# Cosine attention with top-128 routing: seven consecutive tokens per partition, 64x64 transposes, and 128-wide tiles throughout

## The chip, the core and the metric

The kernel runs on one core of a Trainium2 chip, as one launch. The metric is the device time of that launch in microseconds (us). The engines that the text names are TensorE (PE in the profile; PEld is its weight loading), VectorE (DVE), ScalarE (ACT), GpSimd (POOL) and SyncE (SP), which here only issues transfers. SBUF is the on-chip memory and PSUM the memory that TensorE writes.

## The reference

Eight batches, twelve heads, 448 tokens and 64 numbers per head and token. The attention is a softmax over cosine similarities; its result, with the heads side by side (768 numbers per token), goes through a layer in which only the 128 tokens of each batch with the highest score are changed.

```python
q_n = q / (np.linalg.norm(q, axis=-1, keepdims=True) + 1e-06)
k_n = k / (np.linalg.norm(k, axis=-1, keepdims=True) + 1e-06)
scores = np.matmul(q_n, k_n.transpose(0, 1, 3, 2)) / tau          # tau = 0.1
attn = softmax(scores)                                            # over the keys
x = matmul(attn, v)  ->  (8, 448, 768)
for b in range(8):
    s = x[b] @ w_gate
    top = the 128 tokens with the largest s
    h = np.maximum(x[b, top] @ w1, 0.0)                           # w1: 768 x 1024
    out[b, top] = x[b, top] + sigmoid(s[top])[:, None] * (h @ w2) # w2: 1024 x 768
```

448 is three times 128 plus 64. That odd 64 is what the layouts in this case are about.

## The kernel before

Work is done for one pair of heads at a time; there are 48 pairs, six to a batch. The program is scheduled by hand, and each engine runs its instructions in the written order. With `P = 128, NC = 3, NS = 4, T = 64, NB7 = 7, E = 65`:

```python
def load(gi, which, eng):            # q, k or v of a group of up to three pairs
    ...
    if which == 0:                   # q: 1 transfer for tokens 0..383, 2 for the last 64
        eng.dma_start(out=..., in_=src[b, h0:h0+nh, 0:SM, :].rearrange("h (m c) d -> m h (c d)", c=NC))
        for u in range(2):
            eng.dma_start(out=dst[u*T:u*T+T, :, NC], in_=src[b, h0:h0+nh, SM:S, :]...)
        return
    for u in range(2):               # k and v: 4 transfers
        for half in range(2):
            ...
            eng.dma_start(...)
load(0, 0, nc.sync); load(0, 1, nc.scalar)
load(1, 0, nc.sync); load(1, 1, nc.scalar)
load(2, 0, nc.sync); load(2, 1, nc.scalar)
load(0, 2, nc.sync); load(1, 2, nc.sync); load(2, 2, nc.sync)
...
def square(p):  nc.scalar.activation(sq_tiles[p], raw q and k of the pair, AF.Square)    # L198
def sum_pe(p, dst):                  # eight matmuls with the identity: sums of squares   # L205
def sum_dve(p, dst):                 # the rest of the sum                                # L211
def scale(p): ...                    # kn = q, k over their norms, two POOL operations    # L235
def transposes(p, part):
    # part 0: four 64x64 transposes (the last 64 tokens of q, k, two heads)               # L255
    # part 1: six 128x128 transposes                                                      # L250
def qkT_copy(p): nc.vector.tensor_copy(qkT_tiles[p], qkT_ps[:, :W])                       # L269
def scores(i, c, sc=None):           # c = 0..2: one 128-key block, both heads            # L281
                                     # c = 3: the last 64 keys of both heads              # L286
def exps(i, c):                      # exp of a score block on ACT                        # L294, L297
def pv_tails(i):                     # 8 matmuls, 64 rows high                            # L308
    for j in range(NS):
        n = rows(j)                  # 128, and 64 for j = 3
        for u in range(2): matmul(out=o_ps[:n, u, ...], lhsT=ex[r, TAIL, j*P:j*P+n], rhs=vo[r, NC], ...)
def pv(i):                           # 24 matmuls                                         # L320
    for u in range(2):
        for j in range(NS):
            n = rows(j)
            for c in range(NC): matmul(out=o_ps[:n, u, ...], lhsT=ex[:, 2*c+u, j*P:j*P+n], ...)
def pv_evac(i): ...                  # x_b = o_ps / its sum, on DVE                       # L333, L334
def gate(b, j): ...                  # the token score x . w_gate, on DVE                 # L355
def rank_count, pick                 # rank of each token, 0/1 selection, on DVE          # L401, L410
def select(b):                       # 8 matmuls; for j = 3 with 64 rows                  # L420
def gather(b, part):                 # 24 matmuls in two parts; for j = 3 with 64 rows    # L456
def ffn1, ffn2                       # the two layers for the 128 chosen tokens           # L470, L479

for i in range(N + 1):               # the main loop: pair i, and the end of pair i - 1
    scores(i, 0); scores(i, 1)
    pv_tails(i - 1); pv(i - 1)
    exps(i, 0); exps(i, 1); square(...)
    run(i, "D1"); pv_evac(i - 1); run(i, "A"); run(i, "D2")   # D: gate, rank, pick; A: PE work
    scores(i, 2)
    transposes(i + 1, 0); transposes(i + 1, 1); qkT_copy(i + 1)
    sc = ps_sc.tile([P, 2, 512], FP32, name="sc")             # a pool of two buffers
    sums(sq, sc)                     # sum_pe into sc[:, 1], then sum_dve out of it
    scores(i, 3, sc)                 # into sc[:, 0]
    exps(i, 2); exps(i, 3)
    norms(sq)
    run(i, "C"); scale(i + 2); values(i + 2); run(i, "P2"); run(i, "B")   # B: PE work
```

`run` hands in the pieces of the routed layer of the batch before: gates at pairs 0 to 3 of the following batch, ranks at pair 5, gather and the two layers over pairs 6 to 10.

Of the kernel before, what the change touches and what calls it, by code (L numbers as in the profile page):

```python
# [17 lines left out]
def kernel(  # L18
# [51 lines left out]
    def rows(j):  # L70
        return P if j < NC else T
# [10 lines left out]
    while sum(NORMS[-1]) < N:  # L82
# [4 lines left out]
    raw = [(const.tile([P, 2, 3, 8, Dh], FP32, name=f"qk_raw{n}"),  # L87
            const.tile([P, 3, 8, Dh], FP32, name=f"v_raw{n}")) for n in range(NRAW)]

    def load(gi, which, eng):  # L90
        g0, gn = GROUPS[gi]
        b, hp = divmod(g0, HP)
        h0, nh = 2 * hp, 2 * gn
        qk, vr = raw[gi % NRAW]
        src = (q, k, v)[which]
        dst = vr[:, :gn] if which == 2 else qk[:, which, :gn]
        if which == 0:
            eng.dma_start(
                out=dst.rearrange("p g (u c) d -> p (g u) (c d)", c=4)[:, :, :NC * Dh],
                in_=src[b, h0:h0 + nh, 0:SM, :].rearrange("h (m c) d -> m h (c d)", c=NC))  # L100
            for u in range(2):
                eng.dma_start(
                    out=dst[u * T:u * T + T, :, NC],
                    in_=src[b, h0:h0 + nh, SM:S, :].rearrange(
                        "(g h) p d -> p g h d", h=2)[:, :, u])
            return


        for u in range(2):
            for half in range(2):  # L110
                n = NS if half == u else NC
                b0 = 0 if u == 0 else NB7 - n
                t0 = 0 if half == u else NS * T
                eng.dma_start(
                    out=dst[half * T:half * T + T, :, b0:b0 + n]
                    .rearrange("p g c d -> p g (c d)"),
                    in_=src[b, h0:h0 + nh, t0:t0 + n * T, :].rearrange(
                        "(g h) (p c) d -> p g h (c d)", h=2, c=n)[:, :, u])
# [7 lines left out]
    load(2, 1, nc.scalar)  # L126
    load(0, 2, nc.sync)
    load(1, 2, nc.sync)
    load(2, 2, nc.sync)
# [8 lines left out]
    nc.vector.memset(o_ps[T:, :, NC * E:NS * E], 1.0)  # L138
# [6 lines left out]
    kn = const.tile([P, 2, NS, P], BF16, name="qkn")  # L145
# [5 lines left out]
    for t in gates + ranks:  # L151
        nc.vector.memset(t, 0.0)
# [5 lines left out]
    for sl, col, base, step, mult in (  # L158
            (slice(0, NC), 0, 0, 0, NC - 1), (slice(0, NC), 1, 0, 1, 1),
            (slice(NC, NS), 0, SM, 0, 0), (slice(NC, NS), 1, 0, 0, 1)):  # L160
        nc.gpsimd.iota(tokc[:, sl, col], pattern=[[step, sl.stop - sl.start]],
                       base=base, channel_multiplier=mult,
                       allow_small_or_imprecise_dtypes=True)
# [9 lines left out]

    nc.gpsimd.tensor_copy(iden_f, iden_b)
    for j in range(NS):
        nc.gpsimd.affine_select(
            out=tie[:, j, :], in_=tie[:, j, :], compare_op=ALU.is_ge,
            fill=-(2.0 ** -126), base=-j * P, pattern=[[1, S]],
            channel_multiplier=-1)
# [12 lines left out]
    def square(p):  # L192
        gi, g = place[p]
        n, m = nplace[p]
        if m == 0:
            ss_tiles[n] = prep.tile([P, 3, 2, NB7], FP32, name="ss")
        sq_tiles[p] = prep.tile([P, 2, NB7 * Dh], BF16, name="sq")
        nc.scalar.activation(  # L198
            sq_tiles[p], raw[gi % NRAW][0][:, :, g].rearrange("p a b d -> p a (b d)")
            [:, :, :NB7 * Dh], AF.Square)  # L200
# [27 lines left out]
    def scale(p, engines=None):  # L228
        gi, g = place[p]
        n, m = nplace[p]  # L230
        qk = raw[gi % NRAW][0]
        rs = rs_tiles[n]
        for eng, b0, nb, o in zip(engines or (nc.gpsimd, nc.gpsimd),
                                  (0, NS), (NS, NC), (0, Dh)):
            eng.tensor_mul(  # L235
                kn[:, :, :nb, o:o + Dh], qk[:, :, g, b0:b0 + nb],
                rs[:, m, :, b0:b0 + nb].rearrange("p a (b o) -> p a b o", o=1)
                .to_broadcast([P, 2, nb, Dh]))

    def values(p):  # L240
        gi, g = place[p]
        nc.gpsimd.tensor_copy(vo_bufs[p % NB][:, :, :Dh], raw[gi % NRAW][1][:, g, :NB7])  # L242
# [3 lines left out]
    def transposes(p, part):  # L246

        def full(a, c):
            o = a * KO + c * P
            nc.tensor.transpose(out=qkT_ps[:, o:o + P], in_=kn[:, a, c], identity=iden_b)  # L250

        def tail(a, u):
            r = slice(u * T, u * T + T)
            o = SM if a == 0 else KT + u * T
            nc.tensor.transpose(out=qkT_ps[r, o:o + T], in_=kn[r, a, NC, :Dh],  # L255
                                identity=iden_b[r, r], tile_position=(u * T, u * T))

        if part == 0:
            for a in range(2):
                for u in range(2):  # L260
                    tail(a, u)
        else:
            for a in range(2):
                for c in range(NC):
                    full(a, c)
# [34 lines left out]

    def pv_tails(i):
        ex = exp_tiles[i]
        vo = vo_bufs[i % NB]
        for j in range(NS):
            n = rows(j)
            for u in range(2):
                r = slice(u * T, u * T + T)
                nc.tensor.matmul(out=o_ps[:n, u, j * E:(j + 1) * E],  # L308
                                 lhsT=ex[r, TAIL, j * P:j * P + n], rhs=vo[r, NC],
                                 start=(j == 0), stop=False, tile_position=(u * T, 0),  # L310
                                 skip_group_check=True)

    def pv(i):
        ex = exp_tiles[i]
        vo = vo_bufs[i % NB]
        for u in range(2):
            for j in range(NS):
                n = rows(j)
                for c in range(NC):
                    nc.tensor.matmul(out=o_ps[:n, u, j * E:(j + 1) * E],  # L320
                                     lhsT=ex[:, 2 * c + u, j * P:j * P + n],
                                     rhs=vo[:, u * NS + c], start=False,
                                     stop=(c == NC - 1), skip_group_check=True)
# [17 lines left out]
    def store_x(b):  # L341
        x_b = x_tiles[b]
        nc.sync.dma_start(out=out[b, :SM].rearrange("(m c) d -> m c d", c=NC),
                          in_=x_b[:, :NC])
        nc.sync.dma_start(out=out[b, SM:S], in_=x_b[:T, NC])
        xh = xp.tile([P, NS, D], BF16, name="xh")
        nc.gpsimd.dma_start(out=xh, in_=x_b)
        xh_tiles[b] = xh

    def gate(b, j, d0=0, d1=D, prev=None, dst=None):  # L350
        n = rows(j)
        if dst is None:
# [3 lines left out]
            out=junk[:n, d0:d1], in0=x_tiles[b][:n, j, d0:d1],  # L356
            in1=wg_b[:n, d0:d1], scale=1.0,
            scalar=0.0 if prev is None else prev[:n, j:j + 1],
            op0=ALU.mult, op1=ALU.add, accum_out=dst[:n, j:j + 1])

    def rank_prep(b):
# [3 lines left out]
            diag, iden_f.rearrange("p (o c) -> p o c", o=1).to_broadcast([P, NS, P]),  # L365
# [32 lines left out]
    def rank_count(b, j):  # L398
        n = rows(j)
        junk = moe.tile([P, S], BF16, name="junk2", bufs=1)  # L400
        nc.vector.scalar_tensor_tensor(  # L401
            out=junk[:n], in0=st[b]["rep"][:n, :S], scalar=st[b]["own"][:n, j:j + 1],
            in1=tie[:n, j, :], op0=ALU.subtract, op1=ALU.is_gt,
            accum_out=ranks[b % 2][:n, j:j + 1])

    def pick(b, j):
        n = rows(j)
        if j == 0:
            st[b]["sel"] = moe.tile([P, NS, CAP], BF16, name="sel")
        nc.vector.tensor_scalar(  # L410
            out=st[b]["sel"][:n, j], in0=iota_r[:n], scalar1=ranks[b % 2][:n, j:j + 1],
            scalar2=None, op0=ALU.is_equal)

    def select(b):
        sel, sg = st[b]["sel"], st[b]["sg"]
        pk = bank()
        for o, w, src in ((0, 2, tokc), (2, 3, sg)):
            for j in range(NS):
                n = rows(j)
                nc.tensor.matmul(out=pk[:, o:o + w], lhsT=sel[:n, j], rhs=src[:n, j],  # L420
# [26 lines left out]
    def gather(b, part, eng="D", big=False, cut=4):  # L447
# [5 lines left out]
        for t in range(t0, t1):  # L453
            for j in range(NS):
                n = rows(j)
                nc.tensor.matmul(out=ps[:, (t - t0) * CAP:(t - t0 + 1) * CAP],  # L456
                                 lhsT=xh[:n, j, t * P:(t + 1) * P], rhs=sel[:n, j],
# [81 lines left out]
    for t in (ga, gb):  # L539
        nc.vector.memset(t, 0.0)  # L540
# [21 lines left out]
    def sums(ps, sc):  # L562
        for m, p in enumerate(ps):
            dst = sc[:, 1, m * SW:(m + 1) * SW]
            sum_pe(p, dst)
            sum_dve(p, dst)
# [9 lines left out]
    for n in (0, 1):  # L576
# [7 lines left out]
        if n == 0:  # L584
            warm(24)
            scale(0, (nc.gpsimd, nc.vector))
            transposes(0, 0)
            transposes(0, 1)
# [8 lines left out]
    for i in range(N + 1):  # L597
# [11 lines left out]
        if live:  # L609
            exps(i, 0)  # L610
            exps(i, 1)
            if i > 0:
                for p in SQ.get(i, []):
                    square(p)
# [9 lines left out]
        if nxt:  # L624
            transposes(i + 1, 0)
            transposes(i + 1, 1)
            qkT_copy(i + 1)
        if live:
            sc = ps_sc.tile([P, 2, 512], FP32, name="sc")
            sq = (SQ[0] if i == 1 else []) + (SQ.get(i, []) if i else [])  # L630
            sums(sq, sc)
            scores(i, 3, sc)
            exps(i, 2)
            exps(i, 3)
            if i == 0:
                for p in SQ[0]:
                    square(p)
            norms(sq)
# [78 lines left out]
```

## Time and profile before

| | before |
|---|---|
| time, median of 2 runs | 403.56 us (401.82 to 405.29) |
| span of the profiled execution | 404.2 us |
| mean granted TensorE clock | 0.76 |
| PE busy | 321.2 us, 79% |
| ACT busy | 209.4 us, 52% |
| DVE busy | 186.4 us, 46% |
| POOL busy | 159.3 us, 39% |
| HBM traffic | 133 GB/s over the span |

Busy is the time in which an engine had an instruction under way. Matmuls overlap one another, so PE's share says that it was seldom without work, not that the array ran at its peak. The granted clock is the share of full speed at which TensorE was let run: a matmul at 0.5 streams its columns half as fast. A line such as "PE a <- DVE b: 41.4, 42, 3.0" in the view of waits says that PE stood idle before line a, 42 times and 41.4 us in all, until b on DVE had ended, 3.0 us at most. In a timeline each row is a run of like instructions: start, length, engine, line, operation, shapes, count; in brackets how long the engine had been idle before it, and what ended that.

### The profile page before, as it was taken

How to read it: one execution, taken by the hardware profiler on the slowest of the kernel's cores; microseconds unless marked ns; L12 is line 12 of the kernel's file. 1: busy time of each engine (PE TensorE's matmuls, PEld its weight loads, DVE VectorE, ACT ScalarE, POOL GpSimd, SP SyncE). 2: the span in 40 equal slices, each digit the busy share in tenths (PEclk: the TensorE clock that was granted, in tenths of full speed). 3: DMA queues.
4: the chain of work that ended last, by engine and by line, in shares of the span. 5: the costliest groups of instructions: out<-in, count | busy, mean ns of one | idle time of the engine just before them, and what ended most of it. 6: DMA issues, size and time to landing. Idle time of an engine off the chain costs nothing.

```text
span 404.2 us, 8840 instructions
## 1 busy us (share of the span) xinstructions
PE 321.2 (79%) x3639; PEld 223.8 (55%) x3639; DVE 186.4 (46%) x481; ACT 209.4 (52%) x317; POOL 159.3 (39%) x227
## 2 busy tenths in 40 slices
PE   3478878896988699796988698876988788889591
PEld 3456545564665367564675466644666466557270
DVE  1123443546435644566345645475346455664410
ACT  1367886665456554674465654654447444633110
POOL 3152655442344622662336423663236324700401
PEclk9578996566589856995599957996589658956866
DMA  7799999995953759093944678193401134110722
GB/s 186 203 250 250 234 206 300 222 250 154 262 115 99 148 186 233 5 216 98 245 108 118 128 233 189 23 222 137 80 2 20 21 133 85 12 28 2 216 39 39
DMA packets 52104, 57.59 MB, mean 142 GB/s; under 512 B 9696, under 2 KB 47584, under 8 KB 51040
## 3 DMA queue, kind: packets, MB, share of 16 engines
q1 hardware_dynamic: 46208, 43.07, 39.5%
q0 software_dynamic: 4128, 12.58, 17.8%
q10 hardware_dynamic: 1728, 1.38, 1.4%
q8 instruction: 28, 0.46, 0.5%
q14 instruction: 12, 0.10, 0.1%
HBM read 39.71 MB, written 14.16 MB: 133 GB/s over the span
## 4 chain that ended last, share of the span: by engine, by line
PE 57%; DVE 25%; DMA 8%; ACT 3%; issue 2%; SPq 2%; POOL 1%; POOLq 0%; ACTq 0%
PE o_ps L320 16%; PE sc L281 7%; PE m_ps L456 7%; PE m_ps L470 6%; DVE junk L355 5%; DVE qkT L269 5%; PE sc L286 5%; DVE x_b L334 4%; PE m_ps L479 4%; PE o_ps L308 3%; DVE sel L410 3%; DMA qk_raw<-in_q_dram 3%; DMA qk_raw<-in_k_dram 2%; PE qkT_ps L250 2%; DVE junk L401 2%; DMA xh<-x_b 2%
## 5 line engine op out<-in xcount | busy, mean ns | idle before, releaser
L235 POOL TENSOR_TENSOR qkn<-qk_raw,rs 128x384 bf16<-128x384 f32 (+1 forms) x95 | 96.7, 1038 | 196.6 <-PE qkT_ps L250 120.9
L294 ACT ACTIVATE expS<-sc 128x896 bf16<-128x896 f32 x144 | 126.5, 914 | 70.8 <-PE sc L281 70.5
L320 PE MATMUL o_ps<-vo,expS 128*128 128x65 bf16 (+1 forms) x1152 | 72.3, 215 | 0.0
L281 PE MATMUL sc<-qkT 64*128 64x448 bf16 x288 | 58.3, 433 | 9.3 <-DVE qkT L269 5.2
L320 PEld LDWEIGHTS <-expS 128*128 128x128 bf16 (+1 forms) x1152 | 57.4, 113 | 11.5
L297 ACT ACTIVATE expS<-sc 128x448 bf16<-128x448 f32 x48 | 26.1, 544 | 71.9 <-PE sc L286 71.9
L286 PE MATMUL sc<-qkT 128*128 128x448 bf16 x48 | 20.7, 431 | 41.4 <-DVE ss L211 41.4
L198 ACT ACTIVATE sq<-qk_raw 128x896 bf16<-128x896 f32 x48 | 45.4, 951 | 12.5 <-DMA qk_raw<-in_k_dram 9.4
L333 DVE RECIPROCAL rden<-o_ps 128x8 f32<-128x8 f32 x48 | 10.0, 208 | 76.3 <-PE o_ps L320 76.3
L205 PE MATMUL sc<-sq,iden_b 128*128 128x112 bf16 x384 | 33.8, 245 | 13.9 <-ACT sq L198 11.3
L281 PEld LDWEIGHTS <-qkT 64*128 64x128 bf16 x288 | 13.0, 99 | 49.5 <-issue 40.4
L205 PEld LDWEIGHTS <-iden_b 128*128 128x128 bf16 x384 | 28.7, 117 | 16.6 <-issue 14.8
L470 PEld LDWEIGHTS <-w_sb 128*128 128x128 bf16 x384 | 31.2, 121 | 10.7 <-issue 10.0
L269 DVE COPY qkT<-qkT_ps 128x960 bf16<-128x960 bf16 x48 | 31.3, 651 | 10.2 <-PE qkT_ps L250 9.9
L334 DVE TENSOR_TENSOR x_b<-o_ps,rden 128x512 f32<-128x512 f32 x48 | 33.2, 691 | 1.7
L355 DVE CUSTOM_DVE_ANT_0 junk<-x_b,wg_b 128x768 bf16<-128x768 f32 (+3 forms) x32 | 30.8, 963 | 0.2
L456 PEld LDWEIGHTS <-xh 128*128 128x128 bf16 x192 | 17.2, 120 | 24.5 <-issue 15.7
L250 PE MATMUL qkT_ps<-iden_b,qkn 128*128 128x128 bf16 x288 | 30.1, 254 | 0.9 <-POOL qkn L235 0.9
L456 PE MATMUL m_ps<-sel,xh 128*128 128x128 bf16 (+1 forms) x168 | 28.5, 301 | 0.0
L308 PEld LDWEIGHTS <-expS 64*128 64x128 bf16 (+1 forms) x384 | 19.8, 110 | 13.1 <-issue 3.8
L470 PE MATMUL m_ps<-xeT,w_sb 128*128 128x128 bf16 x312 | 26.9, 261 | 0.0
L242 POOL CAST vo<-v_raw 128x448 bf16<-128x448 f32 x48 | 26.6, 555 | 0.0
(86 smaller groups left out, 320.0 us busy)
## 6 DMA issues: line engine op xcount, KB each, us to landing
out_dram<-x_b SPq DMA_DIRECT2D x8, 1152.0 KB, 4.4
qk_raw<-in_q_dram SPq DMA_DIRECT2D x15, 576.0 KB, 5.5
xh<-x_b POOLq DMA_DIRECT2D x8, 768.0 KB, 8.7
v_raw<-in_v_dram SPq DMA_DIRECT2D x30, 192.0 KB, 4.7
qk_raw<-in_k_dram SPq DMA_DIRECT2D x28, 192.0 KB, 5.1
v_raw<-in_v_dram SPq DMA_DIRECT2D x30, 144.0 KB, 4.7
qk_raw<-in_k_dram SPq DMA_DIRECT2D x28, 144.0 KB, 5.5
w_sb<-in_moe_w_dram POOLq DMA_DIRECT2D x2, 1536.0 KB, 18.1
```

The source lines that it names most:

```text
L198: nc.scalar.activation(sq_tiles[p], raw[gi % NRAW][0][:, :, g].rearrange("p a b d -> p a (b d)") [:, :, :NB7 * Dh], AF.Square)
L205: nc.tensor.matmul(out=dst, lhsT=iden_b, rhs=sq[:, :, s * D8:(s + 1) * D8], start=(s == 0), stop=(s == Dh // D8 - 1))
L235: eng.tensor_mul(kn[:, :, :nb, o:o + Dh], qk[:, :, g, b0:b0 + nb], rs[:, m, :, b0:b0 + nb].rearrange("p a (b o) -> p a b o", o=1) .to_broa ...
L269: nc.vector.tensor_copy(qkT_tiles[p], qkT_ps[:, :W])
L281: nc.tensor.matmul(out=sc[:, u, :S], lhsT=qkT[r, KO + c * P:KO + (c + 1) * P], rhs=qkT[r, :S], start=True, stop=True, tile_position=(u * D ...
L286: nc.tensor.matmul(out=sc[:, 0, :S], lhsT=qkT[:, KT:W], rhs=qkT[:, :S], start=True, stop=True)
L294: nc.scalar.activation(ex[:, 2 * c:2 * c + 2], sc[:, :, :S], AF.Exp, scale=inv_tau)
L320: nc.tensor.matmul(out=o_ps[:n, u, j * E:(j + 1) * E], lhsT=ex[:, 2 * c + u, j * P:j * P + n], rhs=vo[:, u * NS + c], start=False, stop=(c ...
L334: nc.vector.tensor_mul(x_tiles[b][:, :, 2 * hp * Dh:2 * (hp + 1) * Dh] .rearrange("p j (u d) -> p j u d", u=2), o[:, :, :, :Dh], rden.to_b ...
L355: nc.vector.tensor_tensor_reduce(out=junk[:n, d0:d1], in0=x_tiles[b][:n, j, d0:d1], in1=wg_b[:n, d0:d1], scale=1.0, scalar=0.0 if prev is ...
L456: nc.tensor.matmul(out=ps[:, (t - t0) * CAP:(t - t0 + 1) * CAP], lhsT=xh[:n, j, t * P:(t + 1) * P], rhs=sel[:n, j], start=(j == 0), stop=( ...
L470: nc.tensor.matmul(out=ps[:, f * CAP:(f + 1) * CAP], lhsT=w1_sb[:, t, fc * P:(fc + 1) * P], rhs=xeT[:, t], start=(t == 0), stop=(t == KD - 1))
```

## The change

Every head's 448 tokens are now laid out as 64 partitions with seven consecutive tokens each (t = 7 p + s), the even head of a pair on partitions 0 to 63 and the odd head on 64 to 127. One transfer then brings q, or k, of a whole group, in runs of 1792 bytes. The first transposes have to put the columns where the later matmuls want them, so all of them are 64x64, one for each tensor, slot s and head: 28 for a pair where there were ten. The output rows that were 64 high (the last query block) become 128 high: the block takes queries 320 to 447, so 64 of them are computed a second time, and the matmuls of PV, of the selection and of the gather no longer change their shape. The second copies of those tokens get a rank that selects nothing.

Three things beside the layout change: the last score block is issued before VectorE's part of the sum of squares, the normalization of q and k is one POOL operation and not two, and the loads of the first groups are issued from other queues.

```diff
     def load(gi, which, eng):
-        if which == 0:
-            eng.dma_start(... tokens 0..383 ...)
-            for u in range(2):
-                eng.dma_start(... the last 64 ...)
+        if which < 2:
+            eng.dma_start(
+                out=qk[:, which, :gn].rearrange("p g s d -> p g (s d)"),
+                in_=src.rearrange("(g h) (t s) d -> (h t) g (s d)", h=2, s=NB7))
             return
...
-    load(2, 1, nc.scalar)
-    load(0, 2, nc.sync)
-    load(1, 2, nc.sync)
-    load(2, 2, nc.sync)
+    load(2, 1, nc.sync)
+    for gi in range(3):
+        load(gi, 2, nc.sync)
...
+    def transposes(p):
+        for a in range(2):
+            for s in range(NB7):
                 for u in range(2):
+                    r = slice(u * T, u * T + T)
+                    o = column(a, u, s)
+                    nc.tensor.transpose(out=qkT_ps[r, o:o + T], in_=kn[r, a, s],
+                                        identity=iden_b[r, r],
+                                        tile_position=(u * T, u * T))
...
+    def qc(j):
+        return slice(j * P, j * P + P) if j < NC else slice(S - P, S)
...
-                nc.tensor.matmul(out=o_ps[:n, u, j * E:(j + 1) * E],
-                                 lhsT=ex[r, TAIL, j * P:j * P + n], rhs=vo[r, NC],
+                nc.tensor.matmul(out=o_ps[:, u, j * E:(j + 1) * E],
+                                 lhsT=ex[r, TAIL, qc(j)], rhs=vo[r, NC],
...
-                    nc.tensor.matmul(out=o_ps[:n, u, j * E:(j + 1) * E],
-                                     lhsT=ex[:, 2 * c + u, j * P:j * P + n],
+                    nc.tensor.matmul(out=o_ps[:, u, j * E:(j + 1) * E],
+                                     lhsT=ex[:, 2 * c + u, qc(j)],
...
-                nc.tensor.matmul(pk[:, o:o + w], lhsT=sel[:n, j], rhs=src[:n, j], ...)
+                nc.tensor.matmul(pk[:, o:o + w], lhsT=sel[:, j], rhs=src[:, j], ...)
...
-                                 lhsT=xh[:n, j, t * P:(t + 1) * P], rhs=sel[:n, j],
+                                 lhsT=xh[:, j, t * P:(t + 1) * P], rhs=sel[:, j],
...
-    def sums(ps, sc):
+    def sums(ps, sc, tail=None):
         for m, p in enumerate(ps):
-            dst = sc[:, 1, m * SW:(m + 1) * SW]
-            sum_pe(p, dst)
-            sum_dve(p, dst)
+            sum_pe(p, sc[:, 1, m * SW:(m + 1) * SW])
+        if tail:
+            tail()
+        for m, p in enumerate(ps):
+            sum_dve(p, sc[:, 1, m * SW:(m + 1) * SW])
...
-            sums(sq, sc)
-            scores(i, 3, sc)
+            sums(SQ.get(i, []), sc, lambda: scores(i, 3, sc))
             exps(i, 2)
             exps(i, 3)
```

Left out here: the index tables, the stores of x and the masks of the ranks, which follow the new order of tokens at about the same number of instructions, and in pair 0 of the main loop the squares of pairs 3 and 4, which move from after the last exp of that pair to before the third one.

## The prediction

> **What bounds the kernel now.** I read the page's busy rows and clock row first, then the waits, then one pair in the timeline, then the start.
>
> ```profile
> PE 321.2 (79%) x3639; PEld 223.8 (55%) x3639; DVE 186.4 (46%) x481; ACT 209.4 (52%) x317; POOL 159.3 (39%) x227
> ...
> PEclk9578996566589856995599957996589658956866
> ...
> PE 57%; DVE 25%; DMA 8%; ACT 3%; issue 2%; SPq 2%; POOL 1%; POOLq 0%; ACTq 0%
> ```
>
> PE is the busiest engine and 57% of the chain that ended last; DVE, 46% busy, is a quarter of that chain, so the two take turns. The clock row swings between 9 and 5: the clock's records in the trace are stretches at 1.0 and at 0.5, and the mean of 0.76 means that 48% of the span ran at half speed. The windows view gives 0.50 for 138.5 to 159.0 us and 1.00 for 159.0 to 182.9 us.
>
> ```profile
> PE sc L286 <- DVE ss L211: 41.4, 42, 3.0
> ```
>
> The last score block (L286) stands 41.4 us, 42 times, behind VectorE's sum (L211), although it needs nothing from it: the two share a PSUM buffer. One pair, at half clock:
>
> ```profile
> 189.58 0.32 PE L255 MATMUL qkT_ps<-iden_b,qkn 64*64 64x64 bf16 x4
> ...
> 189.83 0.82 PE L250 MATMUL qkT_ps<-iden_b,qkn 128*128 128x128 bf16 x6
> ...
> 190.44 0.95 PE L205 MATMUL sc<-sq,iden_b 128*128 128x112 bf16 x8
> ...
> 190.76 0.65 DVE L269 COPY qkT<-qkT_ps 128x960 bf16<-128x960 bf16 x1
> ...
> 191.43 0.28 DVE L211 TENSOR_REDUCE ss<-sc 128x14 f32<-128x112 f32 x1
> 191.76 0.53 PE L286 MATMUL sc<-qkT 128*128 128x448 bf16 x1 [0.36 <-DVE ss L211]
> ...
> 192.09 2.70 PE L456 MATMUL m_ps<-sel,xh 128*128 128x128 bf16 x16
> ...
> 194.51 1.02 PE L281 MATMUL sc<-qkT 64*128 64x448 bf16 x4
> ```
>
> Transposes, sums, then DVE's copy and sum in series, then the score block, then 16 gather matmuls, whose starts fill 192.09 to 194.51. The start:
>
> ```profile
> 4.71 9.31 ACTq L114 DMA_DIRECT2D qk_raw<-in_k_dram  x8
> ...
> 14.06 0.95 ACT L198 ACTIVATE sq<-qk_raw 128x896 bf16<-128x896 f32 x1 [9.37 <-DMA qk_raw<-in_k_dram]
> ```
>
> ACT's queue issues k transfers until 14.02 us, and its first square starts at 14.06. The wait is labelled DMA, but it ends with the issuing.
>
> **What the Trainium skill says.** "TensorEngine Tiling (Array Packing)", Key Properties: changing the tiling mode drains the array. The trace agrees: in PV at full clock (single records near 205 us) whole 128x128 matmuls start 32 ns apart, but 122 to 125 ns pass into and out of each run of three 64-column ones; at half clock (near 196 us) 54 and 175 ns. "TensorE: Matmul & The Clock Gate", Weight-path perf modes: fast weight load needs all 128 weights. The 64-column matmuls are indeed no quicker (36 to 53 ns apart), though the trace doesn't separate this from the drain. The same page, Part 3: tiles on different rows run side by side. The trace agrees: 64x64 transposes of two heads start 3 ns apart. Its Part 1: the clock is half or full, by recent PE activity. The two levels are there; a rule for when they change I can't take from this trace.
>
> **The change, part by part.**
>
> *PV (L320, L308).* Full clock: 12 matmuls of one head take 0.60 us (204.73 to 205.33); twelve at 32 ns are 0.38. Two heads save 0.44, less one exit of 0.09 that remains: about 0.3. Half clock: 0.91 a head against 0.65, so about 0.4. The eight tail matmuls lose one of two mode changes, about 0.1. Mean 0.45 us a pair, and 48 pairs: **-22**. PV lies on the path, since DVE's x_b (L334) waits for its end.
>
> *Transposes.* Ten become 28. At full clock a 64x64 pair of heads starts every 53 ns (206.228, 206.281), at half clock every 72. Fourteen such steps are 0.74 and 1.0 us, with the drain behind them 0.87 and 1.2. Before, from the first tail to the first sum: 0.53 at full clock (180.42, six steps of 55 ns from 180.60) and 0.86 at half (189.58 to 190.44). So **+0.34** us of PE time a pair at either clock, 16 us in all. In four pairs of six a gate (0.99 us, L355) stands on DVE between x_b and the qkT copy, and in one the ranks; there PE waits for DVE anyway. I count about a third: **+6**.
>
> *Last score block ahead of DVE's sum.* The 41.4 us don't vanish. PE must still wait for the qkT copy before the next pair, and in the compiled order of the changed kernel ACT's last exp waits for DVE's sum, so the next pair's second score block, which needs that buffer, waits too. What goes is the score block itself between sum and exp: 55.44 to 55.87 at full clock (0.42), 184.72 to 185.34 at half (0.6). Where PE has its own work (gather, layers) this now starts while DVE copies, but at half clock sums and score block (0.85 + 0.37 us) nearly cover copy and sum already (0.65 + 0.28). I take 0.35 us a pair, 42 pairs: **-15**.
>
> *Gather and select.* 16 gathers take 2.41 us at half clock; whole ones at that clock start 107 ns apart, 1.71 us. The other eight (197.65 to 198.74) go from 1.09 to 0.86. About 1.0 us a batch, and 0.15 for select: **-9** over eight.
>
> *POOL.* Two operations (1.21 + 0.86 us) become one of the same 896 elements. POOL is 39% busy and waits 120.9 us for transposes: **0**.
>
> *Loads.* Bytes are the same; three and four transfers become one. In steady state the loads lie beside the compute: **0**. At the start ACT issues two transfers and not twelve, so the first square can start near 6 us. Less than that 8 us may survive, because the 16 DMA engines are over 90% busy from 10 us on (the DMA row has 9s); but 1792-byte runs should not be slower than the 768 and 1024 bytes of now. The first exp (22.25) should come near 13, and pair 1's last exp (35.92), which waits for group 3, near 28: **-8**.
>
> Sum: -22 + 6 - 15 - 9 - 8 = -48, so 356 us. With fewer gaps PE may be granted full speed for longer. One pair without gates costs 4.63 us at full clock (tail exps at 51.24 and 55.87), one with gates 6.54 at half (73.76 to 80.30) and 5.57 at full. If the half-speed share fell from 48% to 40%, 8% of the span would run about 15 to 20% faster: **-6**. That gives **350**.
>
> **Rivals.**
>
> *The transposes become the bound.* If the 72 ns were 106 (loading and streaming 64 columns in turn at half clock) and nothing were hidden, they would cost up to 0.8 us a pair in the half-clock half, and about 30 us instead of 6: 375 to 380. For it: only four in a row have been measured, and 56 instructions now stand in one run. Against it: the second step came at the same 53 or 72 ns in every group I looked at.
>
> *The wait only changes its name.* DVE's chain (x_b 0.69, gate 0.95, copy 0.65, sum 0.27) is untouched, and in gate and rank pairs PE may stand before the qkT copy for what it stood before the sum. Then the third term is near 5 instead of 15, and the time 360 to 365. For it: the longest waits, 3.0 us, are at the ranks, where DVE is the whole cause.
>
> *The clock decides.* If the half-clock pairs, no longer held by DVE, keep PE busy enough, the slow stretches of 20 to 24 us shorten much: at 25% half speed about 20 us less, 330. It can go the other way, too, if a long run of small transposes counts as little activity: then 365 to 370.
>
> *The start is bound by bandwidth.* Then the 8 us go, and the time is 358.
>
> **Range and chances.** The terms that I trust (PV, gather, start) sum to -39; the uncertain ones (order, transposes, clock) lie between about +20 and -35. I predict 350 us, with 328 to 374 eight times in ten. A gain below 2% would need 395 or more, with both PE rivals at once: faster 0.95, within 2% 0.03, slower 0.02.
>
> **What would show each step.** PV starts 32 ns (54 at half clock) apart with no 122 or 175 ns gaps inside; 28 transposes in 0.74 or 1.0 us from first to last start; the line of 41.4 us gone, and new waits of PE's scores for the qkT copy and for ACT's last exp of 20 to 30 us; gather 107 or 55 ns a matmul throughout; the first square near 6 us and the first exp near 13; a mean clock of 0.78 to 0.82. The prediction is wrong if the transposes take over 1.2 us a pair, if the clock falls below 0.74, or if the freed 41 us stand under another name in full.

## The result and the profile after

| | before | after |
|---|---|---|
| time, median of 2 runs | 403.56 us (401.82 to 405.29) | 320.85 us (318.48 to 323.22) |
| ratio | | 0.795, 95% interval 0.766 to 0.824 |
| span of the profiled execution | 404.2 us | 319.3 us |
| mean granted TensorE clock | 0.76 | 0.892 |
| share of the span at half clock | 48% | 21% |

I had predicted 350 us, with 328 to 374. The direction was right and the size too small: 83 us came off, not 54.

The page of the kernel after, with the rows that were shown of before:

```profile
PE 246.7 (77%) x4503; PEld 188.9 (59%) x4503; DVE 184.1 (58%) x476; ACT 206.8 (65%) x317; POOL 158.1 (50%) x183
...
PEclk9989999997999697987889799959995979699697
...
PE 41%; DVE 24%; ACT 17%; DMA 8%; issue 5%; SPq 2%; POOLq 1%; DVEq 0%; ACTq 0%
```

PE has 864 more matmuls and 74.5 us less busy time. Its share of the last chain falls from 57% to 41%, and ACT's rises from 3% to 17%. The clock row has hardly a 5 left. By the clock's records the stretches at half speed are about as many as before (13 for 12), but shorter: 3.4 or 6.8 us each, where most lasted 17 to 24. The waits:

```profile
ACT expS L292 <- DVE ss L206: 47.1, 43, 3.6
...
PEld L276 <- DVE qkT L264: 29.1, 17, 3.9
...
PE sc L276 <- DVE qkT L264: 24.6, 13, 3.7
```

The line of 41.4 us (the last score block behind VectorE's sum) is gone. In its place ACT's last exp waits for that sum, and 13 times PE waits for the qkT copy. Both waits were predicted, at 20 to 30 us: PE's is 24.6, ACT's 47.1. ACT's last exp had stood longer before, for the score block itself:

```profile
ACT expS L297 <- PE sc L286: 71.9, 44, 3.4
```

One pair with a gate and layer work, at full clock:

```profile
150.17 0.63 PE L258 MATMUL qkT_ps<-iden_b,qkn 64*64 64x64 bf16 x28
...
150.98 0.55 PE L200 MATMUL sc<-sq,iden_b 128*128 128x112 bf16 x8 [0.18 <-ACT sq L193]
...
151.37 0.35 PE L281 MATMUL sc<-qkT 128*128 128x448 bf16 x1
...
151.56 1.50 PE L461 MATMUL m_ps<-xeT,w_sb 128*128 128x128 bf16 x24
...
151.59 0.65 DVE L264 COPY qkT<-qkT_ps 128x960 bf16<-128x960 bf16 x1
152.16 0.27 DVE L206 TENSOR_REDUCE ss<-sc 128x14 f32<-128x112 f32 x1
```

Read PE and DVE against each other. PE begins the layer's 24 matmuls (L461) at 151.56, before DVE has even begun its copy at 151.59. Before, at the same point of the loop body (another pair, also with a gate), they began only when copy and sum were over:

```profile
207.76 0.65 DVE L269 COPY qkT<-qkT_ps 128x960 bf16<-128x960 bf16 x1
208.33 0.27 DVE L211 TENSOR_REDUCE ss<-sc 128x14 f32<-128x112 f32 x1
208.65 0.35 PE L286 MATMUL sc<-qkT 128*128 128x448 bf16 x1 [1.07 <-DVE ss L211]
...
208.84 1.50 PE L470 MATMUL m_ps<-xeT,w_sb 128*128 128x128 bf16 x24
```

Where the 84.9 us of the two profiled spans went, by the start of each pair's last exp in the traces: 11.2 by pair 1 (35.92 to 24.72), 12.1 in pairs 2 to 11, 52.7 in pairs 12 to 41 (227.9 to 175.2), 7.4 in pairs 42 to 47 and 1.4 after the last pair.

### The profile page after: what moved, and what is told of

It reads as the page before. It is cut to its first block, busy times and chain, and to the rows that moved or that the text cites. A ratio compares the mean times of both kernels' runs of the same rounds, so it can differ in the third digit from the quotient of the medians.

```text
span 319.3 us, 10375 instructions
## 1 busy us (share of the span) xinstructions
PE 246.7 (77%) x4503; PEld 188.9 (59%) x4503; DVE 184.1 (58%) x476; ACT 206.8 (65%) x317; POOL 158.1 (50%) x183
## 4 chain that ended last, share of the span: by engine, by line
PE 41%; DVE 24%; ACT 17%; DMA 8%; issue 5%; SPq 2%; POOLq 1%; DVEq 0%; ACTq 0%
PE o_ps L316 9%; PE sc L276 7%; ACT expS L289 7%; DVE junk L350 6%; PE m_ps L461 5%; PE sc L200 5%; DMA qk_raw<-in_k_dram 5%; ACT sq L193 4%; PE m_ps L470 4%; ACT expS L292 4%; DVE junk L395 4%; DMA xh<-x_b 4%; DVE qkT L264 3%; DVE x_b L330 3%; PE qkT_ps L258 3%
## 5 line engine op out<-in xcount | busy, mean ns | idle before, releaser
L231 POOL TENSOR_TENSOR qkn<-qk_raw,rs 128x896 bf16<-128x896 f32 (+1 forms) x48 | 92.3, 1922 | 117.3 <-PE qkT_ps L258 94.0
L276 PE MATMUL sc<-qkT 64*128 64x448 bf16 x288 | 51.9, 387 | 33.0 <-DVE qkT L264 24.6
L292 ACT ACTIVATE expS<-sc 128x448 bf16<-128x448 f32 x48 | 26.1, 543 | 47.6 <-DVE ss L206 47.1
L316 PE MATMUL o_ps<-vo,expS 128*128 128x65 bf16 x1152 | 49.2, 202 | 0.0
L316 PEld LDWEIGHTS <-expS 128*128 128x128 bf16 x1152 | 42.9, 103 | 2.9
L258 PEld LDWEIGHTS <-qkn 64*64 64x64 bf16 x1344 | 28.2, 117 | 15.6 <-issue 12.2
L258 PE MATMUL qkT_ps<-iden_b,qkn 64*64 64x64 bf16 x1344 | 34.3, 203 | 3.8 <-POOL qkn L231 1.9
L350 DVE CUSTOM_DVE_ANT_0 junk<-x_b,wg_b 128x768 bf16<-128x768 f32 (+1 forms) x32 | 33.4, 1045 | 0.2
L200 PEld LDWEIGHTS <-iden_b 128*128 128x128 bf16 x384 | 24.2, 105 | 14.1 <-issue 12.1
L461 PEld LDWEIGHTS <-w_sb 128*128 128x128 bf16 x384 | 24.9, 104 | 5.1 <-issue 3.6
L461 PE MATMUL m_ps<-xeT,w_sb 128*128 128x128 bf16 x312 | 22.2, 233 | 3.0 <-issue 2.4
L395 DVE SCALAR_TENSOR_TENSOR junk<-m_ps,own,tie 128x448 bf16<-128x448 f32 (+1 forms) x32 | 21.9, 683 | 0.8
L485 POOL DMA_INDIRECT out_dram<-oe,idx x8 | 13.0, 1630 | 18.6 <-DVE oe L435 8.8
L221 DVE RECIPROCAL rs<-rs 128x42 f32<-128x42 f32 (+2 forms) x18 | 7.0, 387 | 24.7 <-ACT rs L216 20.3
```

The lines of the kernel that those rows point to most:

```text
L200: nc.tensor.matmul(out=dst, lhsT=iden_b, rhs=sq[:, :, s * D8:(s + 1) * D8], start=(s == 0), stop=(s == Dh // D8 - 1))
L231: eng.tensor_mul(kn[:, :, b0:b1], qk[:, :, g, b0:b1], rs[:, m, :, b0:b1].rearrange("p a (b o) -> p a b o", o=1) .to_broadcast([P, 2, b1 - ...
L258: nc.tensor.transpose(out=qkT_ps[r, o:o + T], in_=kn[r, a, s], identity=iden_b[r, r], tile_position=(u * T, u * T))
L276: nc.tensor.matmul(out=sc[:, u, :S], lhsT=qkT[r, KO + c * P:KO + (c + 1) * P], rhs=qkT[r, :S], start=True, stop=True, tile_position=(u * D ...
L292: nc.scalar.activation(ex[:, TAIL], sc[:, 0, :S], AF.Exp, scale=inv_tau)
L316: nc.tensor.matmul(out=o_ps[:, u, j * E:(j + 1) * E], lhsT=ex[:, 2 * c + u, qc(j)], rhs=vo[:, u * NS + c], start=False, stop=(c == NC - 1) ...
```

## The experiments

The first question was whether the clock made the difference between my sum and the result (Theory A), or whether the terms of the sum were too small (Theory B). Medians below are of four runs; the ratios are to the kernel before, timed beside each set (medians of 399 to 406 us). Executions of one kernel differ by up to 4%, the longer ones mostly at a lower clock, and where that matters the range is given.

### Idle PE filled, nothing else

```diff
             sums(sq, sc)
+            if i >= HP:
+                fill(45 if i % HP == HP - 1 else 10)   # zero tile times zero tile, unused columns
             scores(i, 3, sc)
```

> The kernel before with matmuls added that no result uses: in the place where PE waits for VectorE's sum ahead of the last score block, 10 products of a zero tile (45 in the pairs with ranks) into unused columns of the PV buffer, from pair 6 on. Nothing is taken away, no order is changed. Theory A (most of what I missed is the clock: idle gaps of PE let it fall to half speed, and the changed kernel has fewer): mean clock from 0.76 to 0.84 or more, and 370 to 388 us although PE has 600 matmuls more to do. Theory B (the terms of the sum were each too small and the clock is only a bystander): clock at most 0.78 and 403 to 415 us.

375.28 us, ratio 0.939 (0.927 to 0.950), at a clock of 0.942. The clock row of its page:

```profile
PEclk9599999999999999999999999998998889989766
```

Compare it with the row of before, full of 5 and 6: PE has 665 matmuls more and the kernel is 25 us faster. So in the kernel before the clock really is lost in PE's idle gaps, and holding it is worth about 25 us. That is Theory A's mechanism, but 25 us do not make 83.

### The new order alone

```diff
+    def sums(ps, sc, tail=None):        # sum_pe, then tail(), then sum_dve
...
-            sums(sq, sc)
-            scores(i, 3, sc)
+            sums(sq, sc, lambda: scores(i, 3, sc))
```

> The kernel before with one part of the change: the last score block is issued before VectorE's part of the sums. By my prediction's third term -15 us, so 388, with the clock where it was. Theory A: the gap that cools the clock is this one, so the clock rises to 0.80 or more and the time falls to 370 to 380. Theory B: 385 to 392 and clock 0.75 to 0.77.

355.28 us, ratio 0.885 (0.876 to 0.894): 45 us from moving one group of instructions, three times my term and over what either theory expected. The profiled execution was the longest of the four (360.9 us), at a clock of 0.834; the others had 0.846 to 0.866. Its waits show the names change:

```profile
ACT expS L297 <- DVE ss L211: 54.9, 42, 4.6
...
PE sc L281 <- DVE qkT L269: 26.4, 12, 4.5
```

Pairs that ran wholly at full clock in both traces can be compared without the clock. From one last exp to the next, in pairs 12 to 41, the mean of those pairs at each place in the batch (between the two exps lie, at place 2, the first layer's first half; at 3 its second half; at 4 the second layer; at 5 the rank products and the ranks):

| place in the batch | before, idle PE filled | new order alone | gain |
|---|---|---|---|
| 2 | 6.56 us | 5.46 us | 1.10 |
| 3 | 6.37 | 5.15 | 1.22 |
| 4 | 6.83 | 6.00 | 0.83 |
| 5 | 7.72 | 7.00 | 0.72 |

In pairs without layer work (4 and 5 of the whole) the gain is 4.63 to 4.24 us, 0.39, which is the 0.42 that I had read. The rest, 0.4 to 0.8 us at places 2 to 4, I put down to the layer work, which no longer stands behind DVE: the two stretches of timeline above show it for one pair each.

### The new order at a high clock

> The kernel before with the last score block ahead of VectorE's sums, and idle PE filled with unused products of a zero tile: 45 at the end of each pair with ranks and 4 at the end of every other pair, from pair 6 on, so that the clock stays high (0.90 or more). Against it stands the kernel before with the same kind of filling and the old order (375 us at a clock of 0.94). If the order's 45 us were mostly clock, the two filled kernels lie within 10 us of each other, 365 to 375. If the order is worth what it seems at an equal clock (about 1.0 us a pair in the pairs with layer work, 0.4 in the others, 35 us in all), it comes to 335 to 350.

```diff
         run(i, "B")
+        if i >= HP:
+            fill(45 if i % HP == HP - 1 else 4)
```

351.47 us at a clock of 0.924. Against the filled kernel with the old order (375.28) that is 24 us, between the two expectations. Some filling now stands on the path: the same pairs at places 2, 3 and 5 take 5.69, 5.36 and 7.31 us, each 0.2 to 0.3 more than without filler. With the old order the filler costs such pairs nothing (6.37, 6.83 and 7.72 us at places 3, 4 and 5, against 6.37, 6.83 and 7.71 in the kernel before). So 24 us is, if anything, too little for the order at an equal clock, with the reserve that the two were timed in different sets. Of its 45 us, about half or more is the order and the rest comes with the clock; I can't divide it more finely than that.

### The order undone in the changed kernel

> The changed kernel with that one part undone: VectorE's sums are issued ahead of the last score block again. Theory B: +15 us, 336. Theory A: more than that, 340 to 352, and a clock below 0.86 instead of 0.89.

346.25 us, ratio 0.863 (0.854 to 0.871), clock 0.874. The old wait is back in full:

```profile
PE sc L281 <- DVE ss L206: 41.6, 43, 3.3
```

Against the changed kernel (321.89 in the set below) this is 24 us. The time lies in Theory A's range, but the clock fell only from 0.892 to 0.874, less than it asked for: here most of the time is lost in the wait itself.

### PV narrow again

```diff
-        return slice(j * P, j * P + P) if j < NC else slice(S - P, S)
+        return slice(j * P, j * P + P) if j < NC else slice(SM, S)   # out=o_ps[64:, ...], column tile 64
```

> The changed kernel with the last query block of PV 64 columns wide again (128x64 and 64x64 tiles on output rows 64 to 127), all else as it is. Theory B: +22 us by my first term, 343, clock unchanged within 0.01. Theory A: much of it is the clock: the drains are gaps too, so 345 to 355 and a clock of 0.84 to 0.87.

347.66 us, 26 us over the changed kernel. The four runs are far apart: the fastest, 339.84 us at a clock of 0.867, is 18 us over it, and the other three, 345.69 to 350.06 us at 0.837 to 0.854, are 24 to 28. The profiled execution is the longest of them, at 0.85. Its groups by form, for the PV matmuls (busy us, then the mean length of one in ns, which overlaps the next):

```profile
L319 PE MATMUL o_ps<-vo,expS 128*128 128x65 bf16 x864 | 49.5, 208 | 0.0
...
L319 PE MATMUL o_ps<-vo,expS 128*64 128x65 bf16 x288 | 29.5, 216 | 0.0
```

A quarter of the matmuls, half as wide, takes 29.5 us, against 49.5 for the other three quarters: 102 ns of busy time each against 57. In the changed kernel all 1152 together take 49.2 us (its page). My 22 us lies within the 18 to 28; that the clock falls in all four runs too (0.837 to 0.867, where the changed kernel has 0.892 to 0.901) fits Theory A.

### Gather narrow, loads split, transposes doubled

These three were timed together with the changed kernel itself.

> The changed kernel itself, unaltered, timed on the same chip as the three below, to have their differences free of a change of chip: 318 to 324 us.

321.89 us (318.75 to 323.34), ratio 0.805 (0.797 to 0.814).

```diff
+                lo = 0 if j < NC else T
-                ... lhsT=xh[:, j, t * P:(t + 1) * P], rhs=sel[:, j]
+                ... lhsT=xh[lo:, j, t * P:(t + 1) * P], rhs=sel[lo:, j]
```

> The changed kernel with the last block of the selection and of the gather 64 rows high again (rows 64 to 127, which hold the real tokens). By my fourth term +9 us. Theory A (gaps cost clock as well): 10 to 14 us and a clock 0.01 to 0.02 lower. Theory B: 7 to 10 us and the clock unchanged.

332.16 us, ratio 0.833 (0.825 to 0.841): 10.3 us, where I had 9. The clock is 0.872 to 0.893 over the four runs, against 0.892 to 0.901, so about 0.01 lower; this doesn't tell the two theories apart.

```diff
-    load(0, 1, nc.scalar); load(1, 1, nc.scalar); load(2, 1, nc.sync)
+    load_k_split(0, nc.scalar); load_k_split(1, nc.scalar); load_k_split(2, nc.scalar)   # four each
```

> The changed kernel with k of the first three groups brought by twelve transfers on ACT's queue again, in place of three; layout and bytes the same. If ACT's issuing held the start, the first square goes from 4.4 us back to near 13, the first last exp of a pair from 17.9 to about 25, and the time rises by 6 to 11 us. If bandwidth held it, under 3 us.

329.72 us, ratio 0.824 (0.817 to 0.832): 7.8 us. The start of its trace and, below, that of the changed kernel:

```profile
3.31 10.46 ACTq L111 DMA_DIRECT2D qk_raw<-in_k_dram  x8
13.82 0.95 ACT L218 ACTIVATE sq<-qk_raw 128x896 bf16<-128x896 f32 x1 [9.25 <-DMA qk_raw<-in_k_dram]
```

```profile
1.21 0.46 ACTq L97 DMA_DIRECT2D qk_raw<-in_k_dram  x1
...
4.40 0.95 ACT L193 ACTIVATE sq<-qk_raw 128x896 bf16<-128x896 f32 x1 [1.95 <-DMA qk_raw<-in_k_dram]
```

The bytes and the layout are the same, in shorter runs; ACT's queue issues up to 13.77 us, and the first square follows at once. So the wait that the profile calls DMA is for the issues that stand ahead of the square in ACT's queue. Each takes only about 0.6 us, 7.3 us for the twelve; for most of the rest (5.75 to 8.93 and 11.62 to 13.17 us) the queue itself stood, before issues that wait for a semaphore. What those semaphores waited for was not taken apart.

```diff
             transposes(i + 1)
+            transposes(i + 1)
```

> The changed kernel with every transpose done twice into the same place: 28 more of 64x64 for a pair, 0.43 us of PE time a pair at full clock by the 32 ns a step seen in its trace. If the transposes lie beside DVE's work in most pairs: +3 to +8 us. If they lie on the path: +20 us (0.43 times 48). A clock that falls below 0.87 would speak for the rival that transposes count as little activity.

351.43 us, ratio 0.878 (0.869 to 0.886), at a clock of 0.887: 29.5 us more, over both expectations. It is not what it looks like:

```profile
105.79 1.07 PE L258 MATMUL qkT_ps<-iden_b,qkn 64*64 64x64 bf16 x56
...
109.41 0.22 PE L305 MATMUL o_ps<-vo,expS 64*128 64x65 bf16 x4
110.73 0.24 PE L305 MATMUL o_ps<-vo,expS 64*128 64x65 bf16 x4 [1.09 <-issue]
```

56 transposes take 1.07 us here, 0.44 more than 28. But in the midst of eight tail matmuls PE stands still for 1.09 us, and the profile finds nothing that it waited for. In the trace after the first 15 us there are 13 stops over 0.25 us ahead of a PE instruction without a wait, 23.2 us in all; the changed kernel has two (4.1 us), or one (1.8 us) in the trace taken beside this run, and the kernel before none. If each us of these stops costs a us, they explain 19 to 21 of the 29.5, and 8 to 10 are left for the transposes themselves. On the path throughout, 28 more would cost 21 (0.44 times 48): more than half lie beside other work. The clock (0.887 against 0.892) says nothing for the rival that transposes count as little activity.

### All four undone

> The changed kernel with four parts undone together: VectorE's sums ahead of the last score block, PV narrow, selection and gather narrow, k of the first groups in twelve transfers on ACT. What stays of the change is the token layout with its one-piece loads, 28 transposes and one POOL operation. If these were worth nothing in themselves, it lands at the time before, 396 to 406 us, and what the four single undoings leave unexplained of the 80 us is that they share gaps and clock. If the layout had a gain of its own that I didn't count: 380 to 392 us. If its 28 transposes cost something that the rest hides: above 408.

405.25 us, ratio 1.025 (1.014 to 1.035). So the token layout, the one-piece loads in steady state, the 28 transposes and the single POOL operation bring nothing by themselves; they cost up to 2.5% (the kernel before ran from 392.5 to 407.7 us beside it). What pays is the four parts, the whole 128-wide matmuls among them; whether these could be had in the old layout was not tried. The four single undoings add to 24 + 26 + 10 + 8 = 68 us (60 with the fastest narrow PV), and all four together cost 83: parts that are undone together lose 15 to 23 us more than the sum. The clock is one thing they share: it is 0.798 here, and 0.85 to 0.89 in the four.

### The clock in the changed kernel

```diff
+            if i % HP == HP - 1 and i > HP:
+                fill(40)
             exps(i, 2)
```

> The changed kernel with 40 products of a zero tile put into PE's longest gap of each batch, the one behind the rank operations, where the clock falls to half in its trace. No result uses them. Theory A (the remaining half-speed stretches come from that gap): clock 0.94 or more and 308 to 316 us. Theory B: 321 to 330.

321.21 us, ratio 0.810 (0.802 to 0.819), at a clock of 0.946. The clock is held, and nothing is won: Theory A's mechanism holds in the gap behind the ranks, but what is gained there does not show in the whole. The pairs 12 to 41 went from 5.77 us each (5.84 in the first trace of the changed kernel) to 5.63; the filled kernel of before went from 7.60 to 6.86.

### Two steps further

The waits of the changed kernel point at DVE's order: the gate stands ahead of the qkT copy.

```diff
-        run(i, "D2")                     # gate, ranks, pick: ahead of scores(i, 2)
...
             norms(SQ.get(i, []))
+        run(i, "D2")
         run(i, "C")
```

> The changed kernel with one more change of order, on VectorE: the gate, rank and pick operations are issued after the qkT copy and the sum instead of ahead of them, so that neither the next pair's scores nor the last exp of this one stand behind them. If what is left is PE and ACT waiting for DVE in those pairs (24.6 us of PE behind the copy, 47.1 us of ACT behind the sum in the changed kernel): 285 to 305 us and a clock over 0.92. If the gates then delay the next pair's x_b by as much: 315 to 325.

304.65 us, ratio 0.764 (0.752 to 0.776), at a clock of 0.941. What it leaves:

```profile
ACT expS L292 <- DVE ss L206: 24.9, 43, 3.2
...
DVE rden L329 <- PE o_ps L316: 19.2, 22, 2.1
```

PE's wait for the qkT copy falls from 24.6 us to 0.9, and ACT's from 47.1 to 24.9.

> The same, and the sums of squares in unused columns of the PV buffer instead of the buffer that the last score block uses, so that the last exp waits for PE alone. On top of the late gates 3 to 10 us less; if PE's sums then wait for x_b to leave the PV buffer, nothing or a loss of up to 10 us.

```diff
-            sum_pe(p, sc[:, 1, m * SW:(m + 1) * SW])
+            sum_pe(p, o_ps[:, m, 320:320 + SW])
```

302.44 us (296.82 to 303.58) at a clock of 0.953. That is not to be told from the 304.65 beside it, although the last exp now waits for PE alone:

```profile
ACT expS L292 <- PE sc L281: 11.9, 23, 2.9
```

Either version beats both kernels.

## Why the prediction was wrong

- **The step that failed is the third: the last score block ahead of DVE's sum.** The mechanism was right and the size too small. I put -15 us on it; it measured 45 us alone in the kernel before and 24 us as the last part in the changed one. I had written that the layer work "now starts while DVE copies", and then set it aside because at half clock PE's own sums nearly cover the copy. In the half-clock pair that I took this from PE waits 0.36 us, but the 42 waits last 0.99 us on average (41.4 / 42), and the full-clock pair shown above waits 1.07. I should have priced each place of the batch: at full clock the gain is 0.7 to 1.2 us at places 2 to 5, against the 0.35 that I took for all.
- **The clock step was mis-sized.** I had -6 us from 48% to 40% at half speed. It went to 21%: I had named this as a rival (25% at half speed, about 20 us) and not taken it. Filling the gaps of the kernel before is worth 0.74 us a pair (7.60 to 6.86), filling those of the changed one 0.14 to 0.21 (5.77 or 5.84 to 5.63). By that I estimate that the clock made 0.5 to 0.6 of the 1.8 us a pair, about a third. It is no cause beside the others: it comes when the gaps go.
- **What stays open.** I missed 29 us (83 against 54). Undone one at a time, the parts show 9 of these in the order and, by the medians, 5 in PV and the gather. Some 15 more show only when the parts are undone together, with the clock at 0.80; how they divide was not measured.
- **Transposes: +6 us was wrong in its numbers.** I took the first step of a run (53 ns) for the steady one. In the changed kernel two 64x64 transposes start every 32 ns at full clock after the first (20.567, 20.599, 20.630 in its records) and every 53 at half. From the first transpose to the first sum, where nothing else holds it, the 28 take 0.56 us at full clock and 0.89 at half; the ten of before took 0.53 and 0.86. So PE's own time grows by 0.03 us a pair and not by 0.34. That the whole pays nothing for them isn't shown: 28 more cost 8 to 10 us beyond PE's stops, and with four parts undone the kernel is up to 2.5% slower than before. That my +6 could fit this would be luck.
- **PV (-22), gather and select (-9) and the start (-8) were right**: 18 to 28, 10.3 and 7.8 us by undoing each. PV's 24 matmuls run at 32 ns from first to last (148.571 to 149.307), with no gap of 122 inside. The first square came at 4.40 us against the 6 that I expected. One reading was wrong: a slice of the DMA row is 10.1 us long, so its 9s begin at 20 us, not at 10.
- **POOL (0) and the loads in steady state (0)** are not contradicted: with all four parts undone, no gain shows.
- **Rivals.** The transposes did not become the bound. The wait did change its name, for about 25 us of PE and 47 of ACT; by my own sign (the freed 41 us under another name in full) that would have been a failure. But ACT had waited longer before (71.9 us, for PE), so the gain was not taken back. The clock decided about a third. The start was bound by the issues in ACT's queue: the same bytes in three transfers let the first square start 9.4 us sooner.

## What to carry to other kernels

When a wait is removed from an in-order engine, price what stands behind it in that queue, place by place of the loop, and not only the instruction that waited: here one score block, after which the next matmuls start 0.19 us later, held back up to 1.5 us of independent matmuls. A short tile in a run of whole ones costs time at both of its ends as well (122 to 125 ns from start to start, where whole ones take 32), so computing 64 columns twice was cheaper here than computing them once. Before crediting the clock, fill the gaps with unused work once in each kernel: that gives a first price in a single run, as far as the filler stays off the path.

## What the runs showed that I had not expected

- PE stops with nothing to wait for: none in the kernel before, 2 stops (4.1 us) in the changed kernel with 28 transposes a pair, 13 (23.2 us) with 56. In the changed kernel's trace both lie next to a 16 KB packet of the instruction queue (120.77 us, stop up to 123.02; 154.33, stop up to 156.79), and that queue carries 35 packets for 28 before. There is one about every 9 us, so that one lies near is weak evidence. The kernel with four parts undone has 28 transposes a pair as well, and as many matmuls as the changed one, but spread over 402 us: it has no such stop. That instructions came too late is my reading; no run took it apart.
- The stores of x became slow. Their 9216-byte packets took 358 ns on average in the kernel before, where they come from 128 partitions. In the changed kernel they come from 64: in the first two batches they took 366 and 371 ns on average, and from the third on 726 to 786. So the 64 partitions alone don't explain it. At the end PE stands 6.6 us for the copy of x where it stood 4.0. It may be part of the 2.5% that the layout costs by itself; this wasn't tried apart.
- At full clock, 64x64 and 64x128 matmuls on the two row halves start 13 to 16 ns apart on average (3 ns within a pair), about half the 32 ns of whole 128x128 ones.
